# All d_ff chunk pairs of the last two tiles by seven block products, and a written order for tiles 3 to 8

## Chip, core and metric

The kernel runs on one core of a Trainium2 chip. The metric is device time in microseconds of one execution, the median of the runs of one program. A profile is one more execution, recorded by the hardware profiler; its span runs from the first to the last instruction. Engines are PE (matrix products), PEld (its weight loads), DVE (vector), ACT (scalar), POOL (GpSimd) and SP (which issues DMAs).

## What is computed

Causal attention by blocks of 64 positions (8 batches, 8 heads, 576 positions, head size 64), then a gated feed-forward block on the 4608 x 512 result, with d_ff = 1536:

```python
scores = scale * np.matmul(q, k.transpose(0, 1, 3, 2))
mask = (pos[:, None] // 64) >= (pos[None, :] // 64)
attn = softmax(np.where(mask, scores, -1e9))
x = np.matmul(attn, v).transpose(0, 2, 1, 3).reshape(4608, 512)

gate = np.maximum(x @ w_gate, 0.0)
val = x @ w_val
out = (gate * val) @ w_out          # float32, 4608 x 512
```

## The kernel before

**Tiles.** The feed-forward block works on nine tiles of 512 rows. Tiles 0 to 7 are the first 512 positions of one batch each, and tile 8 gathers the last 64 positions of all eight batches. x stands transposed (`xT`, for tile 8 `xTt`): 4 x 128 input features on the partitions by 512 rows. d_ff is cut into 12 chunks of 128. For each chunk a gate and a value are made, each by four matmuls of 512 columns into one PSUM bank (L948); ACT applies relu to the gate (L958) and DVE multiplies it with the value (L968, or L995 in tiles 7 and 8), giving a quarter of an `hT` tile.

**Interleaving.** While tile j is in the feed-forward block, attention for batch j + 1 runs beside it in four "visits" of two heads each: scores (L465), exponentials on ACT (L470, L477), corners of the mask set to zero (L1241), products with v (L600, L614), division by the row sums on DVE (L537 to L546), and a DMA transpose on SP's queue into the next `xT` (L647). Loads of batch j + 2 are issued on POOL's queue (L353) and its q and k are transposed by DMA on SP's queue (L362, L119, L120).

**What sets the order.** The feed-forward block is a generator, `ffn_gen`, which yields after each matmul (or two). A table `AT` gives every attention step a place on that sequence; for batches 4 to 7 the places follow from `STEADY` and a base of 144 steps a tile. The main loop advances the generator to a step's place and then issues the step. Each engine runs its instructions in the order issued, and semaphores hold an instruction until its inputs are there. Buffers come from pools that rotate: two PSUM tiles `sc` of two banks each, one bank `one`, three banks `ffnp`.

**Seven block products.** In tiles 2 to 8 the out-projection (L830) treats pairs of chunks as a 2 x 2 block product done with seven products of half blocks instead of eight, of 256 columns. Product 5 and 2 go to banks y and z and 1 to a bank of its own; then 3 is added into y and 4 into z; then 6 and 7 are made. Between them ACT copies banks to SBUF (L868, L879, L885), and DVE and POOL add (L869, L874, L882, L887, L890, L895, L904). The sums of `hT` halves that they need are made by DVE (`make_part`, L789).

In tiles 7 and 8 (`by_pairs`) the gates and values of three pairs of chunks, 2 and 3, 4 and 5, 6 and 7, are made the same way (L1014): gate and value weights and the two halves of x and of the rows form the 2 x 2 blocks. The other six chunks stay plain. A pair takes, with y and z its banks:

- a = copy of y after product 5 and b = copy of z after product 2 (ACT, L1042 and L1044), s: a = a + b (POOL, L1045)
- m: a = product 1 - a (DVE, L1048)
- relu of y after product 3 (ACT), low = copy of z after product 4 (ACT, L1052)
- y: b = y + a after product 6 (DVE, L1055); z: a = z + a after product 7 (DVE, L1057)
- H: one half of the two `hT` chunks = relu x b (DVE, in one pair POOL, L1058); L: the other half = max(a, 0) x low (DVE, L1062)

The sums of x (`x_sums`, L940) and of gate and value weights (`up_sum`, L747) that these products read are made on DVE, the weights' in tiles 5 and 6 into spare buffers.

Of the kernel before, what the change touches and what calls it, by code (L numbers as in the profile page):

```python
# [17 lines left out]
def kernel(  # L18
# [22 lines left out]
    PAIRS = (2, 4, 6)  # L41
    BASE = {0: 0, 1: 512, 3: 896, 2: 1024}
    AW = 1600
    TW = 256

# [78 lines left out]
    class Early:  # L124
# [152 lines left out]
        def pe_mains(self, hp, evac, two=None, ts=(0, 1)):  # L277
            if two is None:
                two = {t: psum_ffn.tile([128, 512], BF, name="ffnp") for t in ts}
# [20 lines left out]
        def pe_tails(self, evac):  # L300

            tq = psum_ffn.tile([128, 4, 64], BF, name="ffnp")
            tk = psum_ffn.tile([128, 4, 128], BF, name="ffnp")
# [13 lines left out]
    def load_qkv(b, which, behind=None):  # L317
        for t in which:
            src = (q, k, v)[t]
            for c in range(NCH):  # L320
# [31 lines left out]
                for dst, part_of in pieces:  # L352
                    ins = nc.gpsimd.dma_start(dst, part_of)  # L353
                    after(ins, behind)
                    behind = None

    bfs = {}

    def dma_transposes(b):
        m, tl = bfs[b, 0], bfs[b, 1]  # L360
        for t in range(2):
# [4 lines left out]
        tails_by_dma(b, tl)  # L366
# [32 lines left out]
    def bank(where, dtype=FP):  # L399

        n = 512 if dtype == FP else 1024
        if where == "sc":
            return psum_sc.tile([128, 2, n], dtype, name="sc")[:, 0, :]
        if where == "one":
            return psum_one.tile([128, n], dtype, name="one")
        return psum_ffn.tile([128, n], dtype, name="ffnp")

    def scores(b, hp, pieces):
        sc = psum_sc.tile([128, 2, 512], FP, name="sc")
# [26 lines left out]
    def thirds():  # L436
        return (
            psum_one.tile([128, 512], FP, name="one"),
            psum_ffn.tile([128, 512], FP, name="ffnp"),
        )  # L440

    def visit(r):
# [3 lines left out]
        first = psum_sc.tile([128, 2, 512], FP, name="sc")  # L446
        second = psum_sc.tile([128, 2, 512], FP, name="sc")
# [26 lines left out]
        def exp_third():  # L474
            for hh in range(2):
# [4 lines left out]

        return exp_third, exp(first, 0), exp(second, 512)

    def last_keys(b):
# [10 lines left out]
        nc.scalar.activation(attnL[b % 2][:, 0:256], last, AF.Exp, scale=scale)  # L494

    def tail_visit(b):

        main = [psum_sc.tile([128, 2, 512], FP, name="sc") for _ in range(2)]
# [34 lines left out]
    def normalise(out, av, x=None):  # L533
        n = av.shape[1]
        rows = av.shape[0]
        recip = sb.tile([128, NCH], FP, name="recip", bufs=4)[0:rows, 0:n]
# [16 lines left out]
    def tail_av(b, g, x):  # L553

        av = psum_ffn.tile([128, 4, 65], FP, name="ffnp")
# [16 lines left out]
        recip = sb.tile([128, NCH], FP, name="recip", bufs=4)  # L572
# [18 lines left out]
    def products_with_v(r, hh, av):  # L591
# [17 lines left out]
        if b >= FIRST:  # L609
# [3 lines left out]
            for c in range(NCH):  # L613
# [9 lines left out]
                )  # L623
        normalise(xnats[r][:, :, 64 * hh : 64 * hh + 64], av, x)

    def head_av(r, hh, where):
        n = 5 if r // 4 >= FIRST else 4
        av = bank(where)[:, 0 : 65 * n].rearrange("q (p e) -> q p e", e=65)
        products_with_v(r, hh, av)
# [25 lines left out]
    store, late = [], []  # L655
# [65 lines left out]

    ups = {}

    def up_sum(n, which):
# [4 lines left out]
        if not ups:  # L729
            ups["free"] = [  # L730
                t[:, 512 * i : 512 * i + 512].rearrange("p (c f) -> p c f", c=2)
                for two in (new_bf(), new_bf())
                for t in two
                for i in range(4)
            ]
# [10 lines left out]
        t = ups[n, which] = ups["free"].pop(0)  # L746
        nc.vector.tensor_tensor(out=t, in0=a, in1=b, op=op)  # L747

    class Sums:
# [3 lines left out]
        def __init__(self, quads):  # L753
            self.quads = quads
            self.two = []
# [52 lines left out]
    def seven_products(j, quads, sums):  # L808
# [33 lines left out]
        early, last = ((0, 1, 2, 3), (4, 5)) if j < B - 1 else ((0, 1, 2, 4), (3, 5))  # L842

        def whole(to, which, new=True, cs=range(6)):
            for p in range(2):
                for c in cs:
                    times(half(to, p), which, p, c, new and (p, c) == (0, 0))
                    if c % 2:
                        yield

        def store_later(hi, n0, ob, p0=0, p1=2):
            if store:
                store.pop()()
            if j < B:
                store.append(lambda: put_block(j, hi, n0, ob, p0, p1))
            else:
                put_block(j, hi, n0, ob, p0, p1)

        y = psum_ffn.tile([128, 512], FP, name="ffnp")
        z = psum_one.tile([128, 512], FP, name="one")  # L860
        for to, which in ((y, 5), (z, 2)):
            yield from whole(to, which, cs=early)
        for to, which in ((y, 5), (z, 2)):
            yield from whole(to, which, new=False, cs=last)
        for q in range(3) if j >= B - 1 else ():
            sums.make_part(q, 1, 0, 2)
        g = sb.tile([128, 512], FP, name="ob", bufs=5)
        nc.scalar.copy(g, y)  # L868
        nc.vector.tensor_tensor(out=g, in0=z, in1=g, op=AX.add)  # L869
        for q in range(3) if j >= B - 1 else ():  # L870
            sums.make_part(q, 2, 0, 2)
        m1 = psum_ffn.tile([128, 512], FP, name="ffnp")
        yield from whole(m1, 1)
        nc.vector.tensor_tensor(out=g, in0=m1, in1=g, op=AX.subtract)  # L874
        if j == B - 1:
            x_sums(B, (1, 3))
        yield from whole(y, 3, new=False)
        c12 = sb.tile([128, 512], FP, name="ob", bufs=5)
        nc.scalar.copy(c12, y)  # L879
        store_later(0, 256, c12)  # L880
        c22 = sb.tile([128, 512], FP, name="ob", bufs=5)
        nc.gpsimd.tensor_tensor(out=c22, in0=g, in1=c12, op=AX.add)  # L882
        yield from whole(z, 4, new=False)
        c21 = sb.tile([128, 512], FP, name="ob", bufs=5)
        nc.scalar.copy(c21, z)  # L885
        store_later(1, 0, c21)
        nc.gpsimd.tensor_tensor(out=g, in0=g, in1=c21, op=AX.add)  # L887
        m6 = psum_ffn.tile([128, 512], FP, name="ffnp")
        yield from whole(m6, 6)
        nc.vector.tensor_tensor(out=c22, in0=m6, in1=c22, op=AX.add)  # L890
        store_later(1, 256, c22)
        if j < B:
            m7 = psum_ffn.tile([128, 512], FP, name="ffnp")
            yield from whole(m7, 7)
            nc.vector.tensor_tensor(out=g, in0=g, in1=m7, op=AX.subtract)  # L895
            store_later(0, 0, g)
        else:
            for p in range(2):
                m7 = psum_ffn.tile([128, 512], FP, name="ffnp")[:, 0:256]
                for c in range(6):  # L900
                    times(m7, 7, p, c, c == 0)
                    if c % 2:
                        yield
                nc.vector.tensor_tensor(  # L904
                    out=half(g, p), in0=half(g, p), in1=m7, op=AX.subtract
                )
                store_later(0, 0, half(g, p), p, p + 1)
# [34 lines left out]
    def ffn_gen():  # L942
        for j in range(B + 1):
# [12 lines left out]
            def relu(gate):  # L956
                gate_sb = sb.tile([128, 512], BF, name="gate_sb", bufs=3)
# [14 lines left out]
            sums = Sums(quads) if j >= SEVEN else None  # L972

            def by_pairs():

                for _ in range(3):
                    quads.append(sb.tile([128, 4, 512], BF, name="hT", bufs=3))  # L980
                gates = {}

                def gate(f):
                    to = psum_ffn.tile([128, 512], FP, name="ffnp")
                    for c in range(4):
                        product(to, 0, c, f)
                        yield
                    gates[f] = relu(to)

                def value(f):  # L990
                    to = psum_ffn.tile([128, 512], FP, name="ffnp")
                    for c in range(4):
                        product(to, 1, c, f)
                        yield
                    nc.vector.tensor_tensor(  # L995
                        out=quads[f // 4][:, f % 4], in0=gates[f], in1=to, op=AX.mult
                    )

                def times(to, n, which, new):
                    i, lo = divmod(PAIRS[n], 4)  # L1000
                    f = slice(128 * lo, 128 * lo + 256)
                    left = {3: wg[i][:, 0:2, f], 4: wv[i][:, 2:4, f]}.get(which)
                    left = ups[n, which] if left is None else left
                    if which in (2, 5):
                        right = x_part(
                            j,
                            slice(0, 2) if which == 2 else slice(2, 4),
                            int(which == 5),
                        )
                    else:  # L1010
                        right = xsum[j, which].rearrange("p (c n) -> p c n", c=2)
                    for k in range(2):
                        for c in range(2):
# [801 lines left out]
```

## Time and profile before

| | us |
|---|---|
| median of 3 runs (351.35 to 353.55) | 351.77 |
| the profiled execution's span | 350.5 |
| PE busy in it | 339.8 |
| DVE busy | 225.5 |
| ACT busy | 185.2 |
| POOL busy | 153.8 |

Busy time is the time in which an engine has an instruction under way; matmuls are pipelined, and the records' ends are modelled. The span is 1.3 us below the median. A group's line gives the line of code, engine, operation, output and inputs, shapes and count, then busy time, the mean duration in ns, and the idle time before it with what ended it. A line of the chain of waits gives start, duration and what ran.

### The profile page before, as it was taken

The page shows a single profiled execution, that of the slowest core. Times are in us where ns is not written, and L with a number is a line of the kernel's source. Part 1 is how long each engine was busy: PE and PEld are TensorE (multiplying, and loading weights), DVE is VectorE, ACT ScalarE, POOL GpSimd, SP SyncE. Part 2 cuts the span into 40 slices and gives each one's busy share as a digit, 9 for nine tenths or more (in the row PEclk, how much of TensorE's full clock was granted, in tenths as well). Part 3 has the DMA queues.
Part 4 walks back from the last instruction along what each step waited for, and adds up shares of the span by engine and source line. Part 5 has one row for each costly group of instructions (what it writes and reads, how often), then busy time and mean ns, then how long its engine had stood idle before and what let it go on. Part 6 is the DMA issues. An engine that isn't in the chain of part 4 may idle for free.

```text
span 350.5 us, 8275 instructions
## 1 busy us (share of the span) xinstructions
PE 339.8 (97%) x3210; PEld 208.2 (59%) x3254; DVE 225.5 (64%) x564; ACT 185.2 (53%) x297; POOL 153.8 (44%) x194
## 2 busy tenths in 40 slices
PE   8999999999999999999999999999999999999994
PEld 3544455545445568545855576556755687687673
DVE  4853455667529784467547772668567867986892
ACT  5933766687235862666355545555366525423521
POOL 2767556576598902590149203950300022213213
PEclk9999999999999999999999999999999999999999
DMA  8999989999999994999459974999510031003005
GB/s 240 295 353 373 352 224 248 222 148 155 184 185 153 144 182 98 138 147 169 62 134 141 104 135 123 127 131 150 121 47 17 16 94 50 2 2 121 1 2 120
DMA packets 155399, 50.02 MB, mean 143 GB/s; under 512 B 134464, under 2 KB 151744, under 8 KB 155360
## 3 DMA queue, kind: packets, MB, share of 16 engines
q0 software_dynamic: 70528, 8.98, 49.1%
q1 hardware_dynamic: 77520, 32.52, 44.0%
q10 hardware_dynamic: 7312, 8.00, 7.8%
q8 instruction: 25, 0.41, 0.5%
q14 instruction: 14, 0.11, 0.1%
HBM read 37.75 MB, written 9.44 MB: 135 GB/s over the span
## 4 chain that ended last, share of the span: by engine, by line
PE 77%; DMA 14%; POOL 3%; issue 2%; DVE 2%; ACT 1%; SPq 1%; POOLq 0%; ACTq 0%
PE ffnp L948 39%; PE ffnp L830 12%; PE one L830 5%; PE sc L1014 3%; DMA stage<-in_moe_w_out_dram 3%; PE sc L465 3%; DMA xT<-xnat 2%; DMA stage<-in_moe_w_val_dram 2%; PE one L465 2%; DMA stage<-in_v_dram 2%; DMA stage<-in_moe_w_gate_dram 2%; PE ffnp L600 2%; PE one L600 2%; PE ffnp L1181 2%; PE one L1014 2%
## 5 line engine op out<-in xcount | busy, mean ns | idle before, releaser
L958 ACT ACTIVATE gate_sb<-ffnp 128x512 bf16<-128x512 f32 x95 | 57.1, 605 | 74.8 <-PE ffnp L948 66.5
L948 PE MATMUL ffnp<-xT,wg 128*128 128x512 bf16 x338 | 93.0, 379 | 1.7 <-issue 0.6
L948 PE MATMUL ffnp<-xT,wv 128*128 128x512 bf16 x309 | 87.7, 380 | 1.0 <-DVE hT L968 0.3
L968 DVE TENSOR_TENSOR hT<-gate_sb,ffnp 128x512 bf16<-128x512 bf16 x76 | 51.9, 683 | 46.0 <-PE ffnp L948 27.0
L948 PEld LDWEIGHTS <-wv 128*128 128x128 bf16 x384 | 35.4, 98 | 38.2 <-issue 4.6
L470 ACT ACTIVATE attnT<-sc 128x1024 bf16<-128x1024 f32 x56 | 57.0, 1042 | 0.0
L948 PEld LDWEIGHTS <-wg 128*128 128x128 bf16 x384 | 35.7, 98 | 35.0 <-issue 1.7
L882 POOL TENSOR_TENSOR ob<-ob 128x512 f32<-128x512 f32 x7 | 9.6, 1370 | 101.7 <-ACT ob L879 53.3
L830 PEld LDWEIGHTS <-stage 128*128 128x128 bf16 x420 | 40.3, 98 | 6.0
L789 DVE TENSOR_TENSOR stage<-hT 128x512 bf16<-128x512 bf16 (+2 forms) x82 | 37.8, 493 | 0.9
L600 PEld LDWEIGHTS <-attnT 128*128 128x128 bf16 x640 | 26.7, 98 | 11.9 <-DVE attnT L1241 0.9
L830 PE MATMUL ffnp<-stage 128*128 128x256 bf16 x252 | 31.4, 273 | 0.0
L353 POOL DMA_DIRECT2D v_bf<-in_v_dram x30 | 24.1, 869 | 6.1 <-DVE recip L537 2.6
L477 ACT ACTIVATE attnT<-one 128x512 bf16<-128x512 f32 (+1 forms) x28 | 15.0, 536 | 21.1 <-PE ffnp L465 21.1
L353 POOL DMA_DIRECT2D q_bf<-in_q_dram x20 | 17.9, 907 | 16.7 <-DVE hT L968 9.7
L1181 PE MATMUL ffnp<-wo,hT 128*128 128x512 bf16 x91 | 23.2, 379 | 0.3
L465 PEld LDWEIGHTS <-kTm 64*128 64x128 bf16 x384 | 11.0, 94 | 15.1 <-issue 7.9
L1045 POOL TENSOR_TENSOR ob<-ob 128x512 f32<-128x512 f32 x6 | 7.6, 1266 | 23.2 <-ACT ob L1044 23.2
L353 POOL DMA_DIRECT2D k_bf<-in_k_dram x20 | 17.8, 927 | 0.0
L830 PEld LDWEIGHTS <-hT 128*128 128x128 bf16 x168 | 16.4, 98 | 1.9
L465 PE MATMUL sc<-qTm,kTm 64*128 64x512 bf16 (+1 forms) x168 | 16.8, 305 | 0.0
L879 ACT COPY ob<-ffnp 128x512 f32<-128x512 f32 x7 | 4.1, 585 | 22.1 <-PE ffnp L830 22.1
(194 smaller groups left out, 556.0 us busy)
## 6 DMA issues: line engine op xcount, KB each, us to landing
out_dram<-ob ACTq DMA_DIRECT2D x28, 256.0 KB, 2.3
stage<-in_moe_w_val_dram SPq DMA_DIRECT2D x6, 512.0 KB, 8.7
stage<-in_moe_w_gate_dram SPq DMA_DIRECT2D x6, 512.0 KB, 8.2
stage<-in_moe_w_out_dram SPq DMA_DIRECT2D x6, 512.0 KB, 10.5
q_bf<-in_q_dram POOLq DMA_DIRECT2D x20, 128.0 KB, 4.2
k_bf<-in_k_dram POOLq DMA_DIRECT2D x20, 128.0 KB, 5.2
v_bf<-in_v_dram POOLq DMA_DIRECT2D x20, 128.0 KB, 7.0
stage<-in_v_dram SPq DMA_DIRECT2D x19, 128.0 KB, 5.5
```

The source lines that it names most:

```text
L353: ins = nc.gpsimd.dma_start(dst, part_of)
L465: nc.tensor.matmul(o, kTm[b % 2][head_of(hh), c, hp, :], qT, start=True, stop=True)
L470: return lambda: nc.scalar.activation(at[:, :, lo : lo + 512], sc, AF.Exp, scale=scale)
L477: nc.scalar.activation(at[:, hh, 1024 : 1024 + w], third[hh][:, 0:w], AF.Exp, scale=scale)
L600: nc.tensor.matmul(av[:, p, :], at[:, col : col + 128], v_bf[b % 2][:, c, h, :], start=(p == 0), stop=(c == p), skip_group_check=True,)
L789: nc.vector.tensor_tensor(out=out.rearrange("p (c n) -> p c n", c=m), in0=a, in1=b, op=op)
L830: nc.tensor.matmul(to, sums.of(c)[which][:, 128 * p : 128 * p + 128], right, start=first, stop=(c == 5), skip_group_check=True,)
L948: nc.tensor.matmul(to, (wg, wv)[t][f // 4][:, c, 128 * (f % 4) : 128 * (f % 4) + 128], x[:, c], start=(c == 0), stop=(c == 3),)
L958: nc.scalar.activation(gate_sb, gate, AF.Relu)
L968: nc.vector.tensor_tensor(out=h, in0=gate_sb, in1=val, op=AX.mult)
L1014: nc.tensor.matmul(to[:, 256 * k : 256 * k + 256], left[:, c, 128 * k : 128 * k + 128], right[:, c], start=new and (k, c) == (0, 0), stop= ...
L1181: nc.tensor.matmul(op, hT[f][:, 128 * s : 128 * (s + 1)], wo[f // 4][:, f % 4, n0:n1], start=(f == 0), stop=(f == 11),)
```

## The change

**Pairs.** `PAIRS` becomes `(0, 2, 4, 6, 8, 10)`: in tiles 7 and 8 all six pairs of chunks are made by seven block products, and no plain chunk is left there. The order of the operations in a pair is free now: each is a word of a list. `p53` is two matmuls of product 3 of pair 5, `p5y` that pair's y, and so on. s and H of every pair are on POOL, m, y, z and L on DVE.

**Weight sums.** There are thirty for fifteen. Those for products 6 and 7 are written in place over the weights, in tile 6; the others go to `stage` and to `attnT` buffers. `ON_POOL` puts fifteen of them on POOL.

```diff
-        t = ups[n, which] = ups["free"].pop(0)
-        nc.vector.tensor_tensor(out=t, in0=a, in1=b, op=op)
+        if which in (6, 7):
+            t = a
+        else:
+            where, i, k = UP_MEM[n][(5, 2, 1).index(which)]
...
+        ups[n, which] = t
+        on(f"U{n}{which}").tensor_tensor(out=t, in0=a, in1=b, op=op)
```

**Out-projection.** Products 3 and 4 come first, then 1, 5, 2, 6, 7 in tile 2 (`OUT_2`) and freely in the later lists. The signs of the additions change with it; `oc` and `od`, the two additions that POOL did, are subtractions now, on POOL or DVE by `ON_POOL` (DVE in tiles 7 and 8, and for `oc` in tiles 3 to 6).

```diff
+            if which == 3:
+                st["y"] = psum_ffn.tile([128, 512], FP, name=slot("ffnp"), bufs=1)
+                yield from whole(st["y"], 3, cs=chunks)
+            elif which == 4:
+                st["z"] = psum_one.tile([128, 512], FP, name="one")
+                yield from whole(st["z"], 4, cs=chunks)
+            elif which in (5, 2):
+                yield from whole(st["y" if which == 5 else "z"], which, new=False)
...
+            elif name == "oc":
+                st["c22"] = ob()
+                add(f"{j}oc", st["c22"], st["g"], st["c21"], AX.subtract)
+            elif name == "od":
+                add(f"{j}od", st["g"], st["g"], st["c12"], AX.subtract)
+            elif name == "o6":
+                add("", st["c22"], st[6], st["c22"], AX.add)
+            elif name == "o7":
+                add("", st["g"], st["g"], st[7], AX.subtract)
```

**Written order.** The generator runs for tiles 0 to 2 alone. From tile 3 on, `program(j)` carries out a list word by word: `g`, `v` plain gates and values (one matmul a word), `r` relu, `h` the product, `M` two matmuls of an out-projection product, `p` parts of a pair, `o` and `S` the out-projection's additions and stores, `s` sums of `hT`, `X` and `Y` sums of x, `U` weight sums, `A` a visit's scores, `E` its exponentials, `C` corners, `V` products with v, `N` the division, `T` the transpose into `xT`, `K` the last keys, `l`, `w`, `d` loads and transposes of a later batch. Tiles 3 to 6 share a list, in which `ONLY` keeps the weight sums to tiles 5 and 6. The end of tile 6's list, part of tile 7's and the end of tile 8's:

```diff
+    ORDER_3_6 = """
...
+        M5 oy M2*2 oz w3 w4 T1 N30 M6*3 M7*2 l10 d3 N31 U57 U46 M6 om U07 M6 M7 U51 U25
+        T3 S1 U47 U36 M7*2 S0 M7 w5 oc o6 od U56 o7 S2
+    """
+    ORDER_7 = """
+        p12 X1 X3 X4 X6 Y1 p12 p1b p15*2 p1a p02*2 p05*2 p0b p11 p01 p11 p13 p1s p0a p0s
...
+        s1101 p44*2 p4l p52*2 p5b p46*2 p53 p47 p51 p53 p5r p3L p47 p51 p54 p4y p4z p54
+        p5l M1 p56*2 M6 p5s p5m s1112 p5y p57*2 p5z M3 M1 M4*2 M3 p4H p4L p5L p5H s1201
+        s2101 M4*3 M3*2 M4 s2112 M3*2 M1*4 s2012 s1012 oa M5 s1001 M5 s2001 M5*2 ob om
...
+    ORDER_8 = """
...
+        oz M5*3 oy S0 s1212 M7 M6*2 s2212 M7 M6*4 oc od o7a Sa S1 o6 S2 M7*3 o7b Sb
+    """
...
+        for j in range(3, B + 1):
+            do, end = program(j)
+            for item in ORDER[j].split():
+                t, _, times = item.partition("*")
+                if j not in ONLY.get(t, (j,)) or (t[0] in "lwd" and j == B - 2):
+                    continue
+                for _ in range(int(times or 1)):
+                    do(t)
+            end()
```

**Named buffers.** Instead of a rotation of two `sc`, three `ffnp`, five `ob` and three `gate_sb`, each allocation names one buffer, by a sequence written out for each (`SLOTS`, `slot`); `PAIR_BANK` and `AV_BANK` name the kind of bank for pairs and for products with v. The reciprocal's tile has two buffers instead of four.

```diff
-            gate_sb = sb.tile([128, 512], BF, name="gate_sb", bufs=3)
+            gate_sb = sb.tile([128, 512], BF, name=slot("gate_sb"), bufs=1)
```

Loads of q, k and v are issued one at a time (`load_qkv` yields), as are the four transposes of a batch (`dma_transpose`).

More of the change, by code (lines that the diff above doesn't have):

```diff
@@ new lines @@
+    """
+    ONLY = {
+        'U01': (6,),
+        'U02': (6,),
+        'U05': (6,),
+        'U06': (6,),
+        'U07': (6,),
+        'U11': (5,),
+        'U12': (5,),
+        'U15': (5,),
+        'U16': (6,),
+        'U17': (6,),
+        'U21': (5,),
+        'U22': (5,),
+        'U25': (5,),
+        'U26': (6,),
+        'U27': (6,),
+        'U31': (5,),
+        'U32': (5,),
+        'U35': (5,),
+        'U36': (6,),
+        'U37': (6,),
+        'U41': (6,),
+        'U42': (6,),
+        'U45': (6,),
+        'U46': (6,),
+        'U47': (6,),
+        'U51': (6,),
+        'U52': (6,),
+        'U55': (6,),
+        'U56': (6,),
+        'U57': (6,),
+        'Y4': (6,),
+    }
@@ L44, with slot @@
     TW = 256
+    slots = {tag: iter(order) for tag, order in SLOTS.items()}
+    def slot(tag):
+        return tag + next(slots[tag])
     consts = ctx.enter_context(tc.tile_pool(name="consts", bufs=1))
@@ L278, in pe_mains @@
             if two is None:
-                two = {t: psum_ffn.tile([128, 512], BF, name="ffnp") for t in ts}
+                two = {t: psum_ffn.tile([128, 512], BF, name=slot("ffnp"), bufs=1) for t in ts}
             for t in ts:
@@ L720, in weight_differences, with on @@
             eng.tensor_tensor(out=d, in0=d, in1=n, op=AX.subtract)
+    def on(name):
+        return nc.gpsimd if name in ON_POOL else nc.vector
     ups = {}
     def up_sum(n, which):
[L729 to L735, printed above, removed]
         i, lo = divmod(PAIRS[n], 4)
@@ L846, in whole @@
                 for c in cs:
-                    times(half(to, p), which, p, c, new and (p, c) == (0, 0))
-                    if c % 2:
+                    times(half(to, p), which, p, c, new and (p, c) == (0, cs[0]))
+                    if cs.index(c) % 2:
                         yield
[L851 to L855, printed above, removed]
-            else:
-                put_block(j, hi, n0, ob, p0, p1)
@@ L859, in seven_products @@
[L859 to L907, printed above, removed]
+        st = {}
@@ new lines, in ob, with products @@
+        def ob():
+            return sb.tile([128, 512], FP, name=slot("ob"), bufs=1)
+        def products(which):
+            if which == 3:
[6 more added lines that the diff above has]
+                yield from whole(st["y" if which == 5 else "z"], which, new=False)
+            elif which == 7 and j == B:
+                for p in range(2):
+                    st[7, p] = psum_ffn.tile([128, 512], FP, name=slot("ffnp"), bufs=1)[:, 0:256]
+                    for c in range(6):
+                        times(st[7, p], 7, p, c, c == 0)
+                        if c % 2:
+                            yield
+            else:
+                st[which] = psum_ffn.tile([128, 512], FP, name=slot("ffnp"), bufs=1)
+                yield from whole(st[which], which)
@@ L942, in ffn_gen @@
     def ffn_gen():
-        for j in range(B + 1):
+        for j in range(3):
             hT = []
@@ L1197, in ffn_gen @@
                 sums.step(12)
-                yield from seven_products(j, quads, sums)
+                some, do = seven_products(j, quads, sums)
+                for what in OUT_2:
+                    if isinstance(what, int):
+                        yield from some(what)
+                    else:
+                        do(what)
+                last_of.append(lambda do=do: do("S3"))
                 continue
```

587 lines of the change are left out of this document (403 added, 184 removed).

## The prediction, made before the changed kernel was run

> **What bounds the kernel now.** I read the summary of engines first, then busy time in windows, one for each tile, and then the chain of waits, which gives the pace of matmuls. (A tile here is one of the nine blocks of 512 rows of the block after attention.)
>
> ```profile
> PE 339.8 (97%) x3210; PEld 208.2 (59%) x3254; DVE 225.5 (64%) x564; ACT 185.2 (53%) x297; POOL 153.8 (44%) x194
> ...
> 241.24:278.39 37.15, 36.78 (x365) 22.73 (x369) 25.90 (x70) 20.16 (x34) 2.99 (x2) 1.00 0.31 65
> 288.47:317.18 28.71, 28.55 (x215) 21.14 (x216) 23.11 (x42) 11.57 (x21) 7.79 (x6) 1.00 0.11 37
> 317.18:345.95 28.77, 28.70 (x216) 20.94 (x214) 21.95 (x39) 11.58 (x21) 7.79 (x7) 1.00 0.12 33
> 345.95:350.50 4.55, 0.00 (x0) 0.00 (x0) 0.38 (x1) 0.00 (x0) 0.36 (x1) 0.88 0.56 145
> ```
>
> The columns are the width, then PE, PEld, DVE, ACT, POOL. The first window is one period of the steady stage (tiles 3 to 6), the next two are tiles 7 and 8, the last is what follows the last matmul. PE leaves 0.37 us idle in a steady period and 0.16 and 0.07 us in tiles 7 and 8, at a granted clock of 1.00, so only fewer columns make it faster. The chain gives the pace, and the order of the end:
>
> ```profile
> 288.47 0.86 PE ffnp L948 x4
> 289.34 0.87 PE sc L1014 x8
> 310.62 2.62 PE ffnp L830 x24
> ...
> 342.87 1.06 POOL ob L882
> 344.21 1.28 POOL ob L887
> 345.51 0.82 DVE ob L904 x2
> ```
>
> A 512-column matmul takes 0.86/4 = 0.215 us of PE, a 256-column one 2.62/24 = 0.109. Check: tile 7 has 48 of the first and 168 of the second (84 in three pairs, 84 in the out-projection), 10.32 + 18.31 = 28.6 against a window of 28.71. PE's own work is the clock of these tiles.
>
> **Matmuls removed.** Three more pairs in tiles 7 and 8 go from 16 matmuls of 512 columns (3.44 us) to 28 of 256 (3.05). A tile then has 252 of 256 columns, 27.5 us, so 1.2 us less, 2.4 in both. Other matmuls only change places. Weight loads are no bound: 98 ns each (costliest groups), and the chain's groups of 256-column matmuls already run at 109 ns with one load each.
>
> **What the vector engine must do in that time.** A pair's m, y, z and L become 24 DVE operations a tile instead of 12, six plain gate products go, H and the sum s go to POOL everywhere, and the two subtractions oc and od of the out-projection come to DVE. Durations, and what happens when operations follow each other:
>
> ```profile
> L1062 DVE SCALAR_TENSOR_TENSOR hT<-ob 128x512 bf16<-128x512 f32 x6 | 4.1, 685 | 0.0
> L1055 DVE TENSOR_TENSOR ob<-sc,ob 128x512 f32<-128x512 f32 x4 | 2.8, 692 | 0.7 <-PE sc L1014 0.5
> L1045 POOL TENSOR_TENSOR ob<-ob 128x512 f32<-128x512 f32 x6 | 7.6, 1266 | 23.2 <-ACT ob L1044 23.2
> L1058 POOL TENSOR_TENSOR hT<-gate_sb,ob 128x512 bf16<-128x512 bf16 x2 | 2.3, 1165 | 4.5 <-DVE ob L1055 4.5
> ...
> 247.37 0.41 DVE L747 TENSOR_TENSOR k_bf<-wg,wv 128x512 bf16<-128x512 bf16 x1
> 247.70 0.41 DVE L747 TENSOR_TENSOR k_bf<-wg 128x512 bf16<-128x512 bf16 x1
> ...
> 305.89 0.69 DVE L1057 TENSOR_TENSOR ob<-one,ob 128x512 f32<-128x512 f32 x1
> 306.50 0.68 DVE L995 TENSOR_TENSOR hT<-gate_sb,ffnp 128x512 bf16<-128x512 bf16 x1
> ```
>
> The left number is a start. Independent operations start 0.61 us apart (305.89, 306.50) though each lasts 0.69, and the short bf16 ones 0.335 apart. One that needs the operation right before it starts 0.82 later (305.07 to 305.89 in the same view, semaphores included). Tile 7 in the new order has 24 for pairs and 6 in the out-projection, 30 x 0.61 = 18.3; 12 sums of 512 elements and 7 sums of x, 19 x 0.335 = 6.4; 6 sums of 256 at about 0.2 = 1.2: 25.9 us. Tile 8: 29 x 0.61, two halves of 0.35, 14 x 0.335, 1.2: 24.3. About eight operations a tile need the one right before, at 0.12 to 0.21 more each, 1.0 at the lower end: 26.9 and 25.3 against 27.5 of PE. DVE, 80% and 76% busy now, keeps 0.6 and 2.2, in all 2.8 us free. ACT gets 27 evacuations a tile of 0.58 to 0.60 us, 16 us of 27.5: it hides. POOL gets 12 operations, 6 x 1.27 + 6 x 1.17 = 14.6: alone it hides too.
>
> **Where DVE and POOL meet.** DVE's sums of x that start while POOL adds are late:
>
> ```profile
> 319.78 1.26 POOL L1045 TENSOR_TENSOR ob<-ob 128x512 f32<-128x512 f32 x1 [2.71 <-ACT ob L1044]
> ...
> 320.47 1.19 DVE L940 TENSOR_TENSOR perm<-xTt 128x512 bf16<-128x512 bf16 x2
> ```
>
> Two such sums alone take 0.335 + 0.41 = 0.75; these took 1.19, the second starting after POOL's end at 321.04. It cost 0.44. At 291.79 the same happened (1.11, 0.36), and at 314.17 POOL waited for DVE (1.56 instead of 1.26, 0.30): 1.1 us in tiles 7 and 8, with no PE idle to show for it. After the change POOL has 12 operations a tile for 6 and DVE some 33 that read two SBUF tiles (18 sums, 6 or 7 of x, 6 L, oc, od) for 21, so meetings are 2 x 33/21 = 3.1 times as many: 3.5 us. 2.8 of it fits into DVE's free time, 0.7 doesn't. Bounds: nothing, and the first rival below.
>
> **The handover inside a tile.** Before, a plain chunk stood between the last pair and the out-projection. Now its third group of product 4 needs H of pair 5. From the last matmul of product 6 of pair 5 in tile 7, PE has eight groups of two (1.74 us) till then; y takes 0.69 with about 0.15 to start, H on POOL 1.17: 2.0. Late by 0.3; if L waits for POOL, 0.5 more. I take 0.4 a tile, 0.8 for both; the ends are 0 and 1.6.
>
> **Moved, at nothing.** (1) Thirty sums of weights for fifteen, half on POOL at about 1.17 us: 12 in tile 6, where POOL is busy 3.0 of 37.15, and 3 in tile 5 next to its loads; DVE idles 11 us there. The ones made in place wait for the last plain product with their weights; behind them on POOL stand od of tile 6 and the first s of tile 7, both needed over 1 us later. If that cover fails, the first pair of tile 7 is late by one operation, 1.2. (2) Tiles 3 to 6: loads are issued one by one on POOL, transposes on SP. xT's last transpose of a tile is now issued some 3 us before the next tile instead of 5 to 7. It lands in 2.4 to 3.6 us (DMA view), and the next tile's scores and three matmuls, 1.3 us, lie before its use: 4.3 against 3.6. Behind it on SP stands only the transpose of the last rows. PE's 0.37 us a period stand where score matmuls change to full ones and back, and stay: no gain; ends -1.5 for all four and the third rival. (3) The out-projection takes products 3 and 4 first in every tile from 2 on: same matmuls. (4) The end: before, the last subtraction of 0.4 us begins at the last matmul's end. Now the 0.69 one of product 6 stands 0.65 us before the end, ahead of it: 0.15 later.
>
> **Sum.** -2.4 + 0.7 + 0.8 + 0.15 = -0.75. The profiled execution has a span of 350.5 and the median of the runs is 351.77, 1.3 outside the span; I keep that. 350.5 - 0.75 = 349.75, so **351.0 us**. A difference under 1% (3.5 us) is about what a measurement of this kernel can't tell from none.
>
> **Rivals.** *POOL and DVE shut each other out, and the pair stage has no room: slower.* In a tile's six pairs PE needs 168 x 0.109 = 18.3 us. If no DVE operation with two SBUF inputs can run beside a POOL one, these must fit one after the other: 14.6 of POOL, 6 L of 0.61, about 9 sums (2.5) and sums of x (0.7 to 2.3), 21.5 to 23: 3.2 to 4.7 over. Groups of the out-projection that stand ready take 1.1. So 2 to 3.6 us a tile, 5.6 for both in the middle; with the handover and the end 5.6 + 0.8 + 0.15 - 2.4 = +4.2: 356.0. It decides once DVE is blocked for more than its 2.8 free plus 1.45 of what PE gained, 4.3 us. For it: the three rows above. Against it: L (f32) is never seen beside POOL, and the pair stages of tiles 7 and 8 can overlap neighbours. The Trainium skill (SBUF — State Buffer, section Who interferes with whom) states this rule: a DVE instruction with two SBUF inputs contends with a GpSimd one that reads SBUF, and the holder keeps the port for the whole instruction. The rows at 320.47 and 314.17 agree for bf16 sums; by the rule L would wait too.
>
> *The whole gain comes through*: meetings and the handover fall into free time; -2.4 + 0.15 gives 349.5. For it: PE lost nothing to three meetings.
>
> *The written order makes tiles 4 to 7 begin late*: xT's last transpose lands a microsecond late at three or four starts, or a weight sum holds POOL: +0.7 each, +2.5: 353.5. Against it is the margin of 0.7 us.
>
> *More than the matmuls is gained*: the steady tiles' 1.5 us go too: 348.0.
>
> **How the numbers follow.** Forecast (350.2 to 352.2) 0.42; whole gain (349.0 to 350.2) 0.17; slower by shutting out (353.5 to 358) 0.27; late starts (352.2 to 355) 0.10; more gained 0.04. The range, 349.0 to 356.2, leaves out the last and half of the slower case, 0.18. One per cent is 348.25 to 355.3. Faster: 0.04, as even 2.4 us is less. Slower: the slower case above 355.3, 0.16, and little else: 0.17. Within: 0.79.
>
> **What would show it.** Right: windows of tiles 7 and 8 of about 28 us each; DVE over 90% busy there; POOL at 14.6; a short wait of PE before product 4's third group; steady periods of 37.15. Wrong: sums or L of over 1 us beside POOL's operations, and PE waiting on DVE inside the pairs (first rival); PE idle at a tile's start before xT lands (third); tiles at 27.5 (second). A steady period that differs by more than 0.5 us would mean that I misjudged the written order.

## The result, and the profile after

The changed kernel takes 368.42 us (median of 4 runs, 367.27 to 373.35) against 351.67 before. It is slower by 16.8 us, far outside the predicted range. The execution profiled first was the 373.35 us one, 5 us over the kernel's other runs, so it is left out of the ratio (1.0459, 95% interval 1.0426 to 1.0491), and everything below is read from a second profile of the same kernel (368.33 us, span 366.3). The windows of that profile, with the columns that the prediction explained: two steady periods, tile 7, tile 8, and what follows the last matmul.

```profile
183.66:220.81 37.15, 36.83 (x368) 22.75 (x368) 24.37 (x69) 20.31 (x33) 14.67 (x18) 1.00 1.50 126
220.81:259.24 38.43, 37.05 (x368) 22.72 (x368) 26.91 (x72) 20.31 (x33) 16.66 (x20) 1.00 1.02 119
290.36:326.51 36.15, 29.69 (x254) 24.27 (x252) 33.30 (x55) 14.95 (x27) 17.46 (x14) 1.00 0.09 29
326.51:360.40 33.89, 29.49 (x254) 24.22 (x251) 31.46 (x53) 14.31 (x27) 16.49 (x12) 1.00 0.10 32
360.40:366.32 5.92, 0.00 (x1) 0.00 (x0) 0.54 (x2) 0.00 (x0) 0.66 (x1) 0.91 0.63 164
```

A steady period is 37.15 us, as before; the one that holds tile 5's weight sums is 1.28 longer. Against the rows of before, tile 7 takes 36.15 instead of 28.71 us, tile 8 33.89 instead of 28.77, the end 5.92 instead of 4.55, and tile 7 begins 1.9 later (290.36 for 288.47): 7.4 + 5.1 + 1.4 + 1.9 = 15.8, the whole difference of the spans (366.3 - 350.5). The clock is 1.00 in both tiles. PE now idles for 6.5 and 4.4 us there, and DVE is the full engine: 33.30 of 36.15 us.

What PE waited for in tiles 7 and 8, from the view of waits (total, times, longest):

```profile
PE sc L1350 <- DVE k_bf L1395: 1.9, 2, 1.8
PE ffnp L1035 <- DVE k_bf L1395: 1.8, 1, 1.8
PE one L1035 <- DVE ob L1384: 1.7, 1, 1.7
PE one L1350 <- DVE ob L1384: 1.7, 1, 1.7
PE one L1035 <- POOL hT L1403: 0.9, 2, 0.6
```

The last is the handover, the wait for H that the prediction put at 0.8. The others are m (L1384) and y (L1395), operations that read a PSUM bank and free it. Their own durations have not changed. What stands ahead of them has. DVE's groups there, each shape apart (busy time, mean ns of one), and after them the sums of hT in the kernel before (tiles 7 and 8, and the short ones from 200 to 275 us):

```profile
L994 DVE TENSOR_TENSOR stage<-hT 128x512 bf16<-128x512 bf16 x24 | 14.7, 648 | 0.0
L1417 DVE SCALAR_TENSOR_TENSOR hT<-ob,q_bf 128x512 bf16<-128x512 f32 x12 | 9.9, 836 | 0.0
L994 DVE TENSOR_TENSOR stage<-hT 128x256 bf16<-128x256 bf16 x12 | 6.5, 558 | 0.1
...
L1395 DVE TENSOR_TENSOR k_bf<-sc,ob 128x512 f32<-128x512 f32 x7 | 4.8, 685 | 0.3
L1156 DVE TENSOR_TENSOR perm<-xT 128x512 bf16<-128x512 bf16 x5 | 4.3, 911 | 0.0
...
L1384 DVE TENSOR_TENSOR ob<-one,ob 128x512 f32<-128x512 f32 x4 | 2.7, 678 | 0.0
```

```profile
L789 DVE TENSOR_TENSOR stage<-hT 128x512 bf16<-128x512 bf16 x14 | 5.2, 420 | 0.3
...
L789 DVE TENSOR_TENSOR stage<-hT 128x256 bf16<-128x256 bf16 x4 | 1.1, 284 | 0.0
```

A sum of hT (L994) of 512 elements took 0.65 us on average instead of 0.42, one of 256 took 0.56 instead of 0.28, L (L1417) 0.84 instead of 0.68, and a sum of x (L1156) 0.91, where one alone takes 0.41 and the mean before was 0.49. The rows with one input from PSUM (L1395, L1384) stand at 0.68, as before. One place, from the timelines of POOL, DVE and PE:

```profile
300.89 3.12 POOL L1379 TENSOR_TENSOR ob<-ob,k_bf 128x512 f32<-128x512 f32 x2
...
300.54 0.94 DVE L1417 SCALAR_TENSOR_TENSOR hT<-ob,q_bf 128x512 bf16<-128x512 f32 x1
301.40 3.23 DVE L994 TENSOR_TENSOR stage<-hT 128x512 bf16<-128x512 bf16 x3
304.56 0.68 DVE L1384 TENSOR_TENSOR ob<-one,ob 128x512 f32<-128x512 f32 x1
...
305.29 0.38 PE L1350 MATMUL one<-perm,stage 128*128 128x256 bf16 x2 [1.72 <-DVE ob L1384]
```

Two s follow each other on POOL from 300.89 to 304.01. Three sums on DVE, 1.08 us if nothing is in their way (two starts 0.335 apart, and 0.41), take 3.23; only the third, which starts after POOL's end, has its normal duration (0.41). m stands behind them in DVE's order, and PE waits 1.72 us for m.

To put numbers on it, I go through DVE's instructions of a pair stage in the trace, from tile 7's first sum of x (tile 8's first m) to the first addition of the out-projection. *Own pace* counts each at the spacing of undisturbed neighbours (0.60, 0.335 or 0.20 us); *held* is by how much an instruction lasts longer than alone (0.69, 0.41 or 0.28); *waits* is the rest. A pause of PE in the text is counted from the last matmul before it, at that matmul's own pace, and its place is that matmul's start; the views, whose ends of matmuls are modelled, print 0.16 less. PE's matmuls in the same stretch, some 196 and 172 at 0.109, take 21.4 and 18.8.

| kernel | tile 7: own + held + waits | tile 8 | sum of both tiles |
|---|---|---|---|
| changed | 20.7 + 7.9 + 1.3 | 18.7 + 5.3 + 0.7 | 54.7 |
| H on DVE | 24.3 + 2.8 + 3.3 | 22.3 + 2.4 + 1.7 | 57.0 |
| H and s on DVE | 27.9 + 0.3 + 3.6 | 25.3 + 0.0 + 1.9 | 59.1 |
| POOL narrow | 20.7 + 0.7 + 1.7 | 18.7 + 0.2 + 0.9 | 42.9 |
| no sums | 16.5 + 3.4 + 5.2 | 14.5 + 1.4 + 4.9 | 45.8 |
| POOL narrow, no sums | 16.5 + 0.6 + 5.3 | 14.5 + 0.2 + 5.1 | 42.0 |
| sums late, tile 5 | 19.7 + 3.4 + 3.3 | 17.7 + 1.4 + 3.1 | 48.5 |
| sums late, H on DVE | 23.3 + 2.9 + 3.0 | 21.3 + 0.9 + 3.0 | 54.3 |

Without its held time the changed kernel's pair stages would need 22.0 and 19.4 us of DVE, beside 21.4 and 18.8 of PE. The experiments below are the other rows.

### The profile page after: what moved, and what is told of

Its sections match the earlier page's. It is cut to its first block, busy times and chain, and to the rows that moved or that the text cites. A ratio compares the mean times of both kernels' runs of the same rounds, so it can differ in the third digit from the quotient of the medians.

```text
span 371.3 us, 8484 instructions
## 1 busy us (share of the span) xinstructions
PE 345.5 (93%) x3289; PEld 216.3 (58%) x3326; DVE 254.8 (69%) x618; ACT 191.7 (52%) x309; POOL 183.6 (49%) x217
## 5 line engine op out<-in xcount | busy, mean ns | idle before, releaser
L618 ACT ACTIVATE attnT<-sc 128x1024 bf16<-128x1024 f32 x56 | 55.6, 1035 | 0.0
L994 DVE TENSOR_TENSOR stage<-hT 128x512 bf16<-128x512 bf16 (+2 forms) x120 | 54.1, 483 | 0.6
L1324 PE MATMUL ffnp<-xT,wg 128*128 128x512 bf16 x192 | 52.1, 379 | 0.3 <-DVE hT L1447 0.3
L1324 PE MATMUL ffnp<-xT,wv 128*128 128x512 bf16 x176 | 49.8, 379 | 1.7 <-issue 0.6
L1447 DVE TENSOR_TENSOR hT<-gate_sb,ffnp 128x512 bf16<-128x512 bf16 x48 | 32.9, 686 | 26.4 <-PE ffnp L1324 21.5
L1319 ACT ACTIVATE gate_sb<-ffnp 128x512 bf16<-128x512 f32 x52 | 30.8, 600 | 25.4 <-PE ffnp L1324 22.5
L1082 POOL TENSOR_TENSOR ob<-ob,ob 128x512 f32<-128x512 f32 x6 | 7.6, 1264 | 70.9 <-DVE ob L1082 63.1
L1164 PE MATMUL ffnp<-xT,wg 128*128 128x512 bf16 x130 | 37.1, 387 | 0.7 <-issue 0.2
L1174 ACT ACTIVATE gate_sb<-ffnp 128x512 bf16<-128x512 f32 x35 | 20.5, 599 | 30.7 <-PE ffnp L1164 24.8
L761 PEld LDWEIGHTS <-attnT 128*128 128x128 bf16 x640 | 26.5, 98 | 12.9 <-ACT gate_sb L1319 1.5
L1035 PE MATMUL ffnp<-stage 128*128 128x256 bf16 x252 | 33.8, 273 | 0.0
L1164 PE MATMUL ffnp<-xT,wv 128*128 128x512 bf16 x108 | 32.0, 386 | 1.9 <-DVE hT L1184 1.8
L1184 DVE TENSOR_TENSOR hT<-gate_sb,ffnp 128x512 bf16<-128x512 bf16 x28 | 19.2, 684 | 17.4 <-PE ffnp L1164 15.8
L1324 PEld LDWEIGHTS <-wg 128*128 128x128 bf16 x192 | 17.9, 98 | 20.3 <-issue 2.6
L1324 PEld LDWEIGHTS <-wv 128*128 128x128 bf16 x192 | 17.9, 98 | 18.8 <-issue 2.1
L1379 POOL TENSOR_TENSOR ob<-ob,k_bf 128x512 f32<-128x512 f32 x12 | 18.0, 1514 | 13.4 <-ACT k_bf L1376 12.8
L1164 PEld LDWEIGHTS <-wv 128*128 128x128 bf16 x144 | 13.3, 99 | 16.8 <-issue 4.4
```

The source lines that it names most:

```text
L618: return lambda: nc.scalar.activation(at[:, :, lo : lo + 512], sc, AF.Exp, scale=scale)
L761: nc.tensor.matmul(av[:, p, :], at[:, col : col + 128], v_bf[b % 2][:, c, h, :], start=(p == 0), stop=(c == p), skip_group_check=True,)
L994: nc.vector.tensor_tensor(out=out.rearrange("p (c n) -> p c n", c=m), in0=a, in1=b, op=op)
L1035: nc.tensor.matmul(to, sums.of(c)[which][:, 128 * p : 128 * p + 128], right, start=first, stop=(c == 5), skip_group_check=True,)
L1164: nc.tensor.matmul(to, (wg, wv)[t][f // 4][:, c, 128 * (f % 4) : 128 * (f % 4) + 128], x[:, c], start=(c == 0), stop=(c == 3),)
L1174: nc.scalar.activation(gate_sb, gate, AF.Relu)
```

## The experiments

*Theory 1*: POOL's operations and DVE's with two SBUF inputs exclude each other; what is held on DVE delays m and y behind it, and PE waits for those. *Theory 2*: DVE simply has too much to do in a fixed order, held or not. *Theory 3*: the written lists and the places of the weight sums in tiles 3 to 6 carry part of the loss.

**The changed kernel again.**

> The changed kernel once more, for a second profile of it. Median 367 to 369, ratio 1.045. If the losses of the first profile (PE idle in the pair stages of tiles 7 and 8, two PE gaps near 107 and 111 us in tile 2, granted clock of 0.5 for 3.4 us after two pauses) belong to the kernel, all of them are here again; what is not here belongs to that one execution.

368.19 us, ratio 1.0464 [1.0448, 1.0480]. The idle of PE in tiles 7 and 8 is here again; the gaps in tile 2 and the drops of the clock are not, so they belong to the first profile's execution.

**H, and H and s, on DVE.** Two kernels, each by the list of what POOL does. The first has no H in it, as shown; the second has no s of tiles 7 and 8 either:

```diff
-        2oc 2od 3od 4od 5od 6od 70H 70s 71H 71s 72H 72s 73H 73s 74H 74s 75H 75s
-        80H 80s 81H 81s 82H 82s 83H 83s 84H 84s 85H 85s U01 U02 U06 U07 U16 U22
+        2oc 2od 3od 4od 5od 6od 70s 71s 72s 73s 74s 75s 80s 81s 82s 83s 84s 85s U01 U02 U06 U07 U16 U22
```

> H of every pair of tiles 7 and 8 on DVE instead of POOL, nothing else: POOL has 12 operations of some 1.27 us fewer, DVE 12 of 0.61 more (7.3 us). Theory 1 (POOL's and DVE's operations with two SBUF inputs exclude each other, and DVE's blocked ones stall PE): half of the meetings go, so half of the some 14 us lost in tiles 7 and 8 comes back less what DVE's own work costs: 360 to 364. Theory 2 (DVE has too much work in a fixed order, whether blocked or not): 7 us more work on the engine that limits, 370 to 376.

> H and s of every pair of tiles 7 and 8 on DVE, nothing else: POOL does no arithmetic there, DVE gets 24 operations of 0.61 more, some 33 us a tile against 27.5 of PE. Theory 1: no DVE operation of over 0.8 us is left in tiles 7 and 8, and what remains is DVE's own work, 33 + 32 us: 358 to 363. Theory 2: 374 to 384, since every operation added to DVE is added to the path.

372.08 us (1.0571 [1.0545, 1.0598]) and 374.24 (1.0636 [1.0579, 1.0692]): slower each time, with theory 2's numbers (370 to 376 and 374 to 384), so theory 1 as I had put it failed. Yet hardly an instruction is held in the second (0.3 us in all), as its groups show:

```profile
L993 DVE TENSOR_TENSOR stage<-hT 128x512 bf16<-128x512 bf16 x24 | 9.3, 416 | 0.0
...
L1416 DVE SCALAR_TENSOR_TENSOR hT<-ob,q_bf 128x512 bf16<-128x512 f32 x12 | 8.0, 683 | 0.0
...
L993 DVE TENSOR_TENSOR stage<-hT 128x256 bf16<-128x256 bf16 x12 | 3.2, 282 | 0.0
```

The table resolves it. Moving the twelve H takes 8.0 us of held time away (13.2 to 5.2) and adds 7.2 of own pace and 3.0 of waits; moving the twelve s takes 4.9 away and adds 6.6. An operation on POOL cost DVE about as much as doing it there (12.9/24 = 0.54 us on average, for 0.60). Both theories describe one sum, own pace plus held time, on an engine that has no room; neither run could tell which part is the change's fault. (The profiled executions of these two also ran 3.4 and 10.2 us at half clock, up to 1.7 and 5.1 us of their time; without these the second could come out between the two theories' numbers.)

**Three pairs only, the rest of the change kept.**

```diff
     ORDER_7 = """
-        p12 X1 X3 X4 X6 Y1 p12 p1b p15*2 p1a p02*2 p05*2 p0b p11 p01 p11 p13 p1s p0a p0s
...
+        g0*4 r0 P X1 X3 X4 p15*2 p1a p12*2 p1b p1s v0*4 h0 X6 X7 p11*2 p1m p13*2 p1r p14*2 p1l
+        g1*4 r1 p16*2 p1y p17*2 p1z p1H p1L v1*4 h1
...
```

> The written order, the out-projection and the 15 sums of weights that three pairs need, but in tiles 7 and 8 only the three pairs of the kernel before (chunks 2 to 7), the other six chunks plain, in an order like that before, H on POOL in one pair, and oc and od on DVE in tiles 7 and 8. If the pairs carry the whole loss (theories 1 and 2): 351 to 354. If the written lists of tiles 3 to 6 and the places of the sums of weights carry part of it (theory 3): 355 or more, with PE gaps before 288 us that the kernel before doesn't have.

357.40 us, 1.0187 [1.0145, 1.0229]: theory 3's number (355 or more), and one PE gap before 288 us is there. Yet eleven of the sixteen microseconds go with the three added pairs. What is left, in its view of waits:

```profile
PE sc L1332 <- DVE ob L1380: 1.4, 2, 0.7
PE ffnp L1306 <- DVE ob L1064: 1.1, 1, 1.1
PE one L743 <- DVE attnT L1510: 1.1, 1, 1.1
```

The last is that gap; it stands in tile 5, and in the changed kernel too. The first two are in tiles 7 and 8, the second where tile 7 begins, in the order that I wrote for this run, so it says nothing of what a well-ordered three-pair kernel would take; it bounds the lists' part from above only.

**POOL's operations made narrow; no sums of hT; both.** All three leave out work (most columns of s and H, the sums of hT, or both), so they serve to find the cause and don't compute the result.

```diff
-                    out=a, in0=a, in1=st.get((n, "b"), z), op=AX.add
+                    out=a[:, 0:64], in0=a[:, 0:64], in1=b[:, 0:64], op=AX.add
...
+                    on(name).memset(h[:, :, 256:512], 0.0)
                     on(name).tensor_tensor(
-                        out=h[:, :, 256:512],
+                        out=h[:, :, 256:288],
```

```diff
         def make_part(self, q, part, k0, k1):
+            if self.late:
+                return
...
+            if self.late:
+                return {
+                    5: h[:, 2 * k, 0:256],
...
```

> POOL's s and H in tiles 7 and 8 work on 64 of 512 columns (the rest of the sum is left out, the rest of H is filled with zeros on POOL by an instruction that reads no SBUF), all else as in the changed kernel: DVE's own instructions are the same. In the second profile of the changed kernel DVE's pair stages (290.8 to 321.6 and 327.8 to 357.1 us) are 21.3 and 21.8 us of its own pace, 8.0 and 5.3 us of instructions that lasted longer than alone, and 3.3 idle. Theory 1 (the excess beside POOL is what PE waits for): no excess is left, 43.1 us of DVE fit beside some 45 of PE, and 10 to 13 us come back: 354 to 358. Theory 2 (DVE's own work and the chain of waits within a pair): 362 to 367.

> The 18 sums of hT halves a tile are left out in tiles 7 and 8 (the products read hT itself), all else as in the changed kernel, POOL's 24 operations among it: DVE has 5.3 us a tile less work, and the instructions that were held most often are gone, though L and the sums of x can still be held. Theory 1: held time falls from 13.3 us to about 5, own work to some 32: 354 to 358. Theory 2: 10.6 us less of DVE's own work: 357 to 360. A chain of waits within a pair that has nothing to do with how busy DVE is would leave 364 or more.

> Both edits of the two runs before: POOL's s and H over 64 columns, and no sums of hT in tiles 7 and 8. Theories 1 and 2 both: DVE is far below PE, so PE sets the time: stalls of the two tiles under 2 us, and 2.4 us of matmuls less than before leave the tail, tile 5 and what is left: 351 to 354. If a chain of waits or the banks of PSUM limit the pair stage, 356 or more.

356.26 us (1.0111 [1.0060, 1.0162]), 359.21 (1.0196 [1.0137, 1.0255]) and 355.08 (1.0093 [1.0070, 1.0117]). The first decides: DVE's instructions are the same, POOL still issues its 24, and 12 us come back, theory 1's number (354 to 358, for 362 to 367). A shorter s or H also comes earlier, but that isn't what came back: DVE's waits in the two pair stages went from 2.0 to 2.6 us. The second run's number is theory 2's (357 to 360), and the third's lies between the two of its expectation; what follows says why. Tiles 7 and 8 of the first run, the end, and two of DVE's groups:

```profile
290.06:319.35 29.29, 28.38 (x254) 24.38 (x252) 26.18 (x55) 14.98 (x27) 8.97 (x20) 1.00 0.11 35
319.35:348.07 28.72, 28.50 (x254) 24.36 (x251) 26.49 (x53) 14.31 (x27) 7.76 (x18) 1.00 0.12 38
348.07:353.92 5.85, 0.00 (x1) 0.00 (x0) 0.54 (x2) 0.00 (x0) 0.66 (x1) 0.84 0.64 166
```

```profile
L994 DVE TENSOR_TENSOR stage<-hT 128x512 bf16<-128x512 bf16 x24 | 9.4, 428 | 0.0
L1419 DVE SCALAR_TENSOR_TENSOR hT<-ob,q_bf 128x512 bf16<-128x512 f32 x12 | 8.2, 693 | 0.0
```

The same 55 DVE instructions that filled 33.30 us of tile 7 now fill 26.18, and 53 that filled 31.46 in tile 8 fill 26.49: the difference of 12.1 us is the held time. Leaving out the sums instead takes both own pace (8.4 us) and held time (8.4) away, and puts 8 us of waits in their place, so that run can't tell the theories apart. With both edits the tiles come to

```profile
290.14:318.70 28.56, 28.19 (x254) 24.45 (x252) 21.19 (x37) 14.99 (x27) 8.65 (x20) 1.00 0.11 36
318.70:347.33 28.63, 28.31 (x254) 24.41 (x251) 21.89 (x35) 14.32 (x27) 7.51 (x18) 1.00 0.12 39
```

so with DVE far from full the tiles still take 28.6 and not 27.5. The trace has one PE gap of 0.49 us in tile 7 and one of 0.46 in tile 8 where the out-projection takes over, and some 0.6 us a tile in small ones. That, the end (5.87) and tile 5 are why even this kernel is slower than the one before.

**Tile 5's three weight sums on DVE.**

```diff
-        80H 80s 81H 81s 82H 82s 83H 83s 84H 84s 85H 85s U01 U02 U06 U07 U16 U22
-        U26 U27 U31 U35 U41 U46 U47 U55 U56
+        80H 80s 81H 81s 82H 82s 83H 83s 84H 84s 85H 85s U01 U02 U06 U07 U16
+        U26 U27 U41 U46 U47 U55 U56
```

> The three weight sums of tile 5 that POOL makes (of pairs 2 and 3) on DVE, nothing else. In the profile of the changed kernel, two of them (224.3 and 225.4 us) hold a sum of hT on DVE for 2.0 us instead of 0.4, two memsets of attention's mask stand behind it, and PE waits 1.2 us for these at 224.9. Theory 1: this gap goes, 1.2 us less, 366.5 to 367.5, and no DVE operation of over 0.8 us between 219 and 230 us. If the gap is due to the order of DVE's work, it stays, or grows by the three sums (1.0 us).

367.32 us, 1.0416 [1.0360, 1.0472], beside 368.19: 0.9 less, which times alone could hardly tell. The timelines can. First the changed kernel's POOL and DVE:

```profile
224.30 1.23 POOL L952 TENSOR_TENSOR stage<-wv 128x512 bf16<-128x512 bf16 x1
225.41 1.41 POOL L952 TENSOR_TENSOR stage<-wg 128x512 bf16<-128x512 bf16 x1
...
223.82 2.00 DVE L994 TENSOR_TENSOR stage<-hT 128x512 bf16<-128x512 bf16 x1
225.88 0.30 DVE L1528 MEMSET attnT<- 64x128 uint32 x2
```

then this one's DVE:

```profile
223.90 0.42 DVE L994 TENSOR_TENSOR stage<-hT 128x512 bf16<-128x512 bf16 x1
224.38 0.30 DVE L1528 MEMSET attnT<- 64x128 uint32 x2
```

One sum was held for 1.6 us, two memsets of attention's mask stood behind it, and products with v waited for these (1.23 us of PE). With the weight sums on DVE the gap is gone, and tile 7 begins at 289.21 instead of 290.36: 1.15 us, theory 1 in another place.

**The sums of hT moved behind the last pair; with tile 5's edit too.** Nothing is left out here.

```diff
-        p0l p06*2 p0y p25 p2a p35 p22*2 p2b p07*2 p1L p0z p35 p0L s0212 p0H s0201 p2s
+        p0l p06*2 p0y p25 p2a p35 p22*2 p2b p07*2 p1L p0z p35 p0L p0H p2s
...
+        p5l M3 p56*2 M3 p5s p5m p5y p57*2 p5z M4*2 p4H p4L p5L p5H s0101 s0112 s1101
+        s1112 s2101 s2112 M3 M4 M3*3 M4*3 oa s0001 s0012 s1001 s1012 s2001 s2012 ob M1*6
+        om M5*6 M2*2 s0201 s0212 s1201 s1212 s2201 s2212 Y3 M2*4 P oy M6*3 oz S1 M6*3 oc
```

> The changed kernel with the 18 sums of hT a tile moved behind the last pair in tiles 7 and 8, where POOL does no arithmetic; the out-projection begins with products 3 and 4 for that, and product 7 stands behind product 6. Nothing is left out. Of the 13.3 us for which DVE's instructions were held in the second profile of the changed kernel, 8.9 are these sums' (4.85 in tile 7, 4.06 in tile 8). Theory 1: they go, and the six to twelve sums that the out-projection then waits for cost up to 1 us a tile: 357 to 361. If POOL's operations then hold other instructions of DVE instead (L, sums of x, which stay where they are): 363 to 367. If the late sums hold PE up more than that: a PE gap of over 2 us behind the last pair.

> The kernel of the run before with the three weight sums of tile 5 on DVE instead of POOL as well: 1.0 to 1.2 us less than that run, and no PE gap of over 1 us in tile 5.

362.50 us (1.0331 [1.0293, 1.0369]) and 360.70 (1.0258 [1.0243, 1.0274]), the first between its two forecasts. Groups of the first:

```profile
L1418 DVE SCALAR_TENSOR_TENSOR hT<-ob,q_bf 128x512 bf16<-128x512 f32 x12 | 10.3, 873 | 0.1
L995 DVE TENSOR_TENSOR stage<-hT 128x512 bf16<-128x512 bf16 x24 | 8.4, 416 | 0.0
```

No sum is held, and held time falls from 13.2 to 4.8 us by the order alone; L is held slightly more (0.87 for 0.84), so the rival that it all passes to L falls. 5.7 us come back. Not all of that is held time: of the 6.5 us by which the span fell (366.3 to 359.8), 4.9 lie in tiles 7 and 8 and 1.5 behind the last matmul (5.9 to 4.4), where this order issues the stores earlier. The tiles gain less than the held time fell because PE now waits behind the last pair: 1.84 us at 312.1 for the L of pair 4 in tile 7 (DVE takes 1.04 for it beside POOL's last H, 0.68 alone), 1.13 at 343.6 for POOL's H itself in tile 8. The second run gained 1.8 more where 1.0 to 1.2 was expected; its trace has the same 1.2 us.

**H on DVE once more, now that the sums are out of the way; then s of two pairs too.**

> The kernel of the run before (sums of hT late, tile 5's three weight sums on DVE) with H of all pairs on DVE in tiles 7 and 8, POOL keeping the six s a tile. DVE gets 12 operations of 0.60 more (7.2 us), and POOL 12 fewer to hold it with. In the last profile 4.8 us of the pair stages are still held time, 1.8 and 1.1 us of PE idle stand behind the last pair, where POOL's last two H hold L. If own pace and held time together set the pair stage (theory 1 with the price of a POOL operation that these runs gave, about 0.55 us of DVE against 0.60 for doing it there): 358.5 to 361.5, with the gaps behind the last pair under 1 us. If the late sums have left room on DVE: 356 to 358.

> The same with s of pairs 0 and 1 of tile 7 on DVE as well, where POOL's s hold two sums of x for 1.1 us each at 291 to 294 us in the profiles before. Two operations of 0.60 take the place of 2.5 us of held time: 1 to 1.5 us less than the run beside it. If the start of tile 7 isn't limited by DVE: no difference.

The edits are those of the first list, with `70s 71s` gone from it too in the second. 366.68 us (1.0425 [1.0394, 1.0457]) and 365.78 (1.0400 [1.0368, 1.0432]): the first was to be 358.5 to 361.5 and missed by 5 us. I had taken the mean price of a POOL operation, 0.55 us of DVE (13.2/24), for the price of each. With the sums gone, the twelve H hold DVE for only 1.0 us (4.8 to 3.8), while they cost 7.2 on DVE itself; the table's sum rises by 5.8, the median by 6.0. So the sum of own pace and held time stands, and the price of a POOL operation is not its own: it depends on what DVE runs beside it. The second run gained 0.9, below the 1 to 1.5 expected: held time at the start of tile 7 went down by 2.2 and own pace up by 1.2.

No version here beats the kernel before; 360.70 is the fastest that computes everything with six pairs. Not tried: letting tile 7's out-projection, where DVE idles, run beside tile 8's pairs.

## Why the prediction was wrong, point by point

- **Matmuls removed, -2.4**: the matmuls are gone, but with DVE unloaded the tiles take 28.56 and 28.63 us, 0.29 less than before in both together. The two gaps of 0.49 and 0.46 us are the handover that I put at 0.4 a tile, though PE waits for L there; in the changed kernel it waits 0.9 us for H in both tiles together, about as forecast. The 0.6 a tile in small gaps I had not counted.
- **What DVE must do**: 26.9 and 25.3 us predicted, 26.18 and 26.49 busy with POOL narrow. The instructions and their paces were right to about 1 us a tile.
- **Where DVE and POOL meet: the step that failed.** "meetings are 2 x 33/21 = 3.1 times as many: 3.5 us. 2.8 of it fits into DVE's free time, 0.7 doesn't." Held time was 13.2 us, and nearly all of it was paid: narrowing POOL's operations gave 12.4 us of span back. It failed twice. The price, 0.30 to 0.44 us, came from three meetings with a single POOL operation each; here two or three sums stand in a row, and with two POOL operations in a row the engines take turns, so that a sum waits for nearly a whole POOL operation (1.1 us each for two of the three at 301.40). And the free time was taken over the tile. It lies in the out-projection (DVE busy 6.3 of the 8.0 us from 321.2), while all 24 POOL operations lie in the pair stage, where DVE without being held already needs 22.0 us beside 21.4 of PE.
- **The first rival** was the right mechanism at the wrong size: +4.2 forecast, +15.8 measured, of which 12.4 are its own. It counted only what cannot overlap, 21.5 to 23 us a tile, and let DVE's other operations run beside POOL. But DVE works in order: m and y stand behind a held sum and cannot pass it, so held time adds to all of DVE's own pace (20.7 + 7.9 + 1.3 = 29.9 in tile 7). My reason against it, that L was never seen beside POOL, was no evidence; seen there, L is held as well (0.84 for 0.68). This is as the Trainium skill (SBUF — State Buffer, section Who interferes with whom) states: a DVE instruction with two SBUF inputs contends with a GpSimd instruction that reads SBUF, one with at most one SBUF input, outside the modes that use two ports, doesn't. The rows of m and y, with one input from PSUM, agree at 0.68 beside POOL.
- **Moved, at nothing**: the steady period without weight sums is 37.15 and no transpose is late, as forecast. The weight sums in tile 5 were not free: I asked whether they delay POOL, not whether they hold DVE, and they cost 1.15 us. Two waits of PE for a product of hT in tile 6, 0.8 us together, are the rest of tile 7's late start. In the trace a held sum stands shortly ahead of each of these products (0.64 instead of 0.28 at 270.79, 0.77 instead of 0.41 at 277.13), while POOL makes weight sums; no run tests it.
- **The end, +0.15**: +1.4. I followed DVE alone. S1 and S2 now come after the subtractions, and the last eight stores are issued between 0.4 us before and 1.7 after the last matmul's end, at 0.6 to 0.8 each on their queues; before, the last was issued 0.9 after. In the last run with POOL's H and late sums all but two of the stores are issued before that end, and it took 4.3.

## What to carry to other kernels

Make the budget of an engine for the stage in which its work must be done, not for the tile, and in order: an instruction that is held takes everything behind it along. An operation given to POOL is paid for by DVE's instructions with two SBUF inputs that stand beside it, between 0.1 and 0.7 us each here; put those into stages in which POOL is quiet, and let instructions that read PSUM stand beside POOL. To tell held time from too much work, narrow the other engine's operations and leave everything else.

## Of the hardware, not expected

- POOL is held as well: s (L1379), 1.26 us alone, took 1.48 on average and up to 1.76 among DVE's sums.
- In or behind pauses of PE of 1.7 to 2.4 us the granted clock fell to 0.5 for 3.41 us, or twice that, in some executions (in the run with H on DVE at 304.6, behind a pause of 2.2 at 302.0) and not in others: the second profile of the changed kernel has four pauses of 1.9 us and no drop behind them, and in the run with H on DVE a pause of 2.9 us at 337 was followed by none. So a PE pause can cost, by an estimate (half of 3.41), up to 1.7 us more than itself, which one profile alone does not show.
